# Attention on TensorE: kv products of two rows at once, 128 columns of k by 128 of v, of whose four quarters two are used

## The chip, the cores and the metric

One core of a Trainium2 chip runs the whole program. The metric is the device time of one execution in microseconds, as the median of several; every run is correct against the reference unless said otherwise. "Before" is the tuned kernel, "after" is the same kernel with the change. All times of single instructions are read from one profiled execution of each kernel.

## The reference, cut to what matters

```python
batch, n_heads, seq, head_dim = (8, 8, 576, 64)
...
kv = np.einsum('bhsd,bhse->bhde', k, v)          # the part that changes
out = np.einsum('bhsd,bhde->bhse', q, kv)
rms = np.sqrt(np.mean(out * out, axis=-1, keepdims=True) + 1e-06)
x = (out / rms * g_norm)                         # to (4608, 512)
# then: a gate, an assignment of tokens to 8 experts in order of their logits,
# and two matrix products per expert (512 -> 1024 -> 512) with a relu between
```

All of it is f32. For each batch and head, kv is a 64x64 matrix, the sum over 576 rows of the outer product of k and v.

## The kernel before

Two heads share the 128 partitions: partitions 0 to 63 (l=0) hold one, 64 to 127 (l=1) the other. A pair of heads is one r, and there are four r in a batch. The 576 rows of a head lie as 64 partitions by 9 rows j, so kv of a head is the sum of 9 matmuls with 64 rows, 64 columns of weights (k) and 64 moving columns (v). The output half is chosen by j, so that four products, 2 l by 2 parities of j, lie in four different 64x64 quarters of the array (in the trace, records of 64x64 that start in fours, 6 to 7 ns apart). The parts of even and odd j are added afterwards.

```python
        kv_ps = psa.tile([P, 2, 512], FT, name="kv_ps", tag="kv")
        def fill(times):      # keeps PE busy, its result is not used
            for _ in range(times):
                nc.tensor.matmul(kv_ps[:, 0, NP * D:512], lhsT=ones_b, rhs=wide[:, 0:512 - NP * D], start=True, stop=True)
        for r in range(NP):
            if r == 2:
                fill(10)
            for j in range(R):
                for l in range(2):
                    ls, cs = slice(l * D, (l + 1) * D), slice(j % 2 * D, (j % 2 + 1) * D)
                    nc.tensor.matmul(kv_ps[cs, l, r * D:(r + 1) * D], lhsT=k_sb[ls, r, j, :], rhs=v_sb[ls, r, j, :],
                                     start=(j < 2), stop=(j >= R - 2))
            if r < 2:
                turn_q(r)     # four transposes of q: the step qt_ps
                yield
        odd = att.tile([D, 2, NP * D], FT, name="odd", tag="odd")
        nc.scalar.copy(odd, kv_ps[D:P, :, 0:NP * D])
        kv = att.tile([D, NP, 2, D], FT, name="kv", tag="kv")
        nc.vector.tensor_tensor(kv..., kv_ps[0:D, :, 0:NP * D]..., odd..., op=AL.add)
        ...                   # t_ps: kv turned, w_ps: kv times the gate, kvx: both side by side
```

The loop that uses kv interleaves with this: for each tile of 128 tokens of batch b a step o_ps (eight matmuls, 64 rows, 128 columns of weights, 72 moving columns), then one piece of the work above for batch b + 1. One tile in nine (4 of 36) takes its two halves from two batches; there the weights are cut into two of 64 columns:

```python
                        parts = [(slice(0, P), halves[0], 2)] if halves[0][0] == halves[1][0] else [
                            (at[n], half, 1) for n, half in enumerate(halves)]
```

## Time and profile before

| | before |
|---|---|
| median time at first | 678.26 us (3 runs, 677.77 to 680.59) |
| span of the profiled run | 676.7 us |
| attention (from 20 us on PE busy 92.7 of 97 us, DMA share 0.92) | to about 117 us |
| search for the assignment (PE busy 18.8 of 46 us, mean clock 0.55) | about 117 to 163 us |
| MoE (PE busy 499.4 of 507 us to 670 us) | from 163 us |
| kv step of one r / of r=2 and 3 | 0.73 / 1.31 us |
| low clock (0.50) in the profiled run | 117.5 to 158.5 us, 3.4 us at 503 us, and the last 6 us |

The page of a profile gives each engine's busy share, digits for 40 slices of the span, and the chain that ended last: the work that, followed back from the end, made the time. The prediction below shows and reads the lines.

### The profile page before, as it was taken

Reading aid. Unit: us, or ns where it says so; the run is one execution under the profiler, and the core shown is the slowest. Engines: PE = TensorE matmul, PEld = TensorE weight load, DVE = VectorE, ACT = ScalarE, POOL = GpSimd, SP = SyncE. Lnnn points to the kernel's source line nnn. Section 1 sums busy time; section 2 is a strip of 40 time slices with the busy share of each in tenths; the row PEclk is TensorE's granted clock in tenths of the full one; section 3 lists DMA queues with packets and bytes.
Section 4 is the critical chain, followed back from the end, with each engine's and each line's share of the span. In section 5 each row is a group of like instructions: output and inputs, shape, how many; then the busy total and the mean of one; then the engine's idle time right before and its main releaser. Section 6 shows DMA issues by size and latency. Waiting matters only on the chain.

```text
span 676.7 us, 13040 instructions
## 1 busy us (share of the span) xinstructions
PE 625.0 (92%) x5123; PEld 488.7 (72%) x5123; DVE 439.9 (65%) x1418; ACT 171.7 (25%) x368; POOL 324.1 (48%) x319
## 2 busy tenths in 40 slices
PE   6999998338999999999999999999989999999994
PEld 4788787224778777877787787868767867887882
DVE  4564768888788888898888884678584155234311
ACT  1665665701210221022103110311123113112300
POOL 1054445002553546264508533846387559928622
PEclk9999999558999999999999999999989999999998
DMA  8999997207208207126207304510460343001002
GB/s 284 306 313 305 333 307 297 109 1 228 92 1 315 74 1 276 43 71 241 79 0 265 125 2 170 170 50 0 171 219 5 120 139 125 1 19 52 1 0 70
DMA packets 41405, 91.03 MB, mean 135 GB/s; under 512 B 3456, under 2 KB 3456, under 8 KB 41344
## 3 DMA queue, kind: packets, MB, share of 16 engines
q1 hardware_dynamic: 34752, 71.31, 30.5%
q0 software_dynamic: 5888, 18.88, 8.3%
q8 instruction: 40, 0.66, 0.4%
q14 instruction: 21, 0.17, 0.1%
q10 hardware_dynamic: 704, 0.02, 0.1%
HBM read 71.32 MB, written 18.87 MB: 133 GB/s over the span
## 4 chain that ended last, share of the span: by engine, by line
PE 82%; DVE 8%; issue 3%; POOL 3%; ACT 1%; DMA 1%; POOLq 0%; SPq 0%; DVEq 0%
PE y_ps L1022 28%; PE h_ps L972 22%; PE h_ps L915 8%; PE o_ps L398 5%; PE y_ps L1037 3%; PE kv_ps L335 3%; PE qt_ps L312 3%; PE t_ps L836 3%; PE kv_ps L327 2%; PE given_ps L558 1%; PE given_ps L554 1%; POOL tw L936 1%; DMA q_sb<-in_q_dram 1%; PE warm_ps L710 1%; DVE over_c L280 1%
## 5 line engine op out<-in xcount | busy, mean ns | idle before, releaser
L972 PE MATMUL h_ps<-xt,w_sb 128*128 128x256 f32 (+1 forms) x640 | 167.1, 412 | 0.1
L972 PEld LDWEIGHTS h_ps<-xt,w_sb 128*128 128x128 f32 x640 | 117.4, 190 | 32.3 <-issue 3.9
L1022 PE MATMUL y_ps<-tw,sh 128*128 128x256 f32 x384 | 86.8, 381 | 0.0
L1022 PEld LDWEIGHTS y_ps<-tw,sh 128*128 128x128 f32 x384 | 71.7, 190 | 9.1
L762 POOL DMA_INDIRECT xg<-x_dram,ids x40 | 38.1, 953 | 67.0 <-DVE held_ps L678 39.6
L950 POOL TENSOR_TENSOR sh<-hid 128x512 f32<-128x512 f32 x32 | 40.6, 1268 | 56.1 <-ACT hid L975 46.8
L975 ACT ACTIVATE hid<-h_ps 128x256 f32<-128x256 f32 (+1 forms) x80 | 32.8, 410 | 132.3 <-PE h_ps L972 124.1
L839 ACT ACTIVATE xt<-t_ps,g_col 128x512 f32<-128x512 f32 (+1 forms) x40 | 25.8, 644 | 143.1 <-PE t_ps L836 142.5
L264 DVE TENSOR_TENSOR over<-mx,held_ps 128x1152 bf16<-128x1152 f32 x42 | 56.9, 1354 | 1.6 <-issue 0.2
L1022 PE MATMUL y_ps<-w_sb,hid 128*128 128x256 f32 x256 | 57.7, 381 | 0.0
L1022 PEld LDWEIGHTS y_ps<-w_sb,hid 128*128 128x128 f32 x256 | 48.2, 190 | 7.0
L843 POOL DMA_INDIRECT out_dram<-y_sb,outs x32 | 32.6, 1020 | 40.8 <-DVE u L992 18.1
L999 POOL TENSOR_TENSOR y_sb<-u,u 128x512 f32<-128x512 f32 x8 | 10.1, 1266 | 78.5 <-issue 63.0
L427 POOL TENSOR_TENSOR xo<-o_sb,inv 128x512 f32<-128x512 f32 x31 | 33.0, 1094 | 28.5 <-ACT sq L404 15.5
L936 POOL TENSOR_TENSOR tw<-w_sb 128x512 f32<-128x512 f32 x32 | 39.9, 1271 | 11.9 <-DMA w_sb<-in_moe_w_dram 11.7
L992 DVE TENSOR_TENSOR y_sb<-y_ps,u 128x512 f32<-128x512 f32 x24 | 16.5, 688 | 39.3 <-PE y_ps L1022 39.1
L915 PE MATMUL h_ps<-sx,tv 128*128 128x288 f32 x144 | 41.2, 423 | 0.7 <-POOL tv L876 0.7
L600 DVE SCALAR_TENSOR_TENSOR held_ps<-n_full,held_ps 32x64 f32<-32x64 f32 x168 | 37.6, 224 | 5.7
L398 PE MATMUL o_ps<-kvx,qt 64*128 64x72 f32 (+1 forms) x640 | 38.7, 269 | 0.9 <-ACT o_sb L405 0.6
L398 PEld LDWEIGHTS o_ps<-kvx,qt 64*128 64x128 f32 (+1 forms) x640 | 33.7, 176 | 5.7 <-issue 2.9
L890 ACT ACTIVATE hid<-hid 128x288 f32<-128x288 f32 x48 | 21.2, 443 | 60.8 <-DVE hid L889 60.3
L992 DVE TENSOR_TENSOR u<-y_ps,u 128x512 f32<-128x512 f32 x24 | 16.4, 685 | 29.5 <-PE y_ps L1022 29.4
(232 smaller groups left out, 1089.2 us busy)
## 6 DMA issues: line engine op xcount, KB each, us to landing
w_sb<-in_moe_w_dram SPq DMA_DIRECT2D x16, 1024.0 KB, 6.2
w_sb<-in_moe_w_dram SPq DMA_DIRECT2D x8, 2048.0 KB, 16.2
k_sb<-in_k_dram SPq DMA_DIRECT2D x16, 576.0 KB, 5.8
v_sb<-in_v_dram SPq DMA_DIRECT2D x16, 576.0 KB, 5.8
q_sb<-in_q_dram SPq DMA_DIRECT2D x16, 576.0 KB, 5.5
x_dram<-xo SPq DMA_DIRECT2D x16, 512.0 KB, 4.1
x_dram<-xo SPq DMA_DIRECT2D x4, 256.0 KB, 4.5
xg<-x_dram,ids POOLq DMA_INDIRECT x40
```

The costliest lines, as they stand in the source:

```text
L264: nc.vector.tensor_tensor(over[:, c0:c1], mx[:, c0:c1].rearrange("p (c o) -> p c o", o=1).to_broadcast([P, c1 - c0, NCAND]), cand[:, 1:NCA ...
L398: nc.tensor.matmul(o_ps[rows_at, rp, (2 * r2 + l) * W:(2 * r2 + l + 1) * W], lhsT=turned_q[bn][ks, l, block // 2:block // 2 + m].rearrange ...
L427: nc.gpsimd.tensor_tensor(xo[:, t], o_sb[:, t, :, 0:D], inv[:, t * H:(t + 1) * H].rearrange("p (h o) -> p h o", o=1).to_broadcast([P, H, D ...
L600: nc.vector.scalar_tensor_tensor(some[g * QP:(g + 1) * QP], in0=n_full.to_broadcast([QP, 2 * QP]), scalar=0.5, in1=one_more, op0=AL.is_gt, ...
L762: tokens = nc.gpsimd.indirect_dma_start(out=xg[0:nr], out_offset=None, in_=x_dram, in_offset=bass.IndirectOffsetOnAxis(ap=ids[0:nr, n:n + ...
L915: nc.tensor.matmul(p_ps, lhsT=left[:, d], rhs=right[:, d], start=d == 0, stop=d == 1)
L936: in_order(nc.gpsimd.tensor_tensor(o[:, m:m + 2], x[:, m:m + 2], y[:, m:m + 2], op=AL.subtract))
L950: in_order(nc.gpsimd.tensor_tensor(o[:, ms], x[:, ms], y[:, ms], op=op))
L972: nc.tensor.matmul(h_ps, lhsT=w1[:, 2 * (d % 2) + d // 2, f * P:(f + 1) * P], rhs=xt[:, d, cs], start=(d == 0), stop=(d == DC - 1))
L975: nc.scalar.activation(hid[:, f, cs], h_ps, ACT.Relu)
L992: nc.vector.tensor_tensor(o, p_ps, u, op=AL.add)
L1022: nc.tensor.matmul(p_ps[:, n], lhsT=left[:, f, n * P:(n + 1) * P], rhs=right[:, f], start=(f == 0), stop=(f == FH - 1))
```

## The change

The intent is fewer and larger matmuls: two rows j at once, so that the weights are 128 columns (k of j and j+1) and 128 columns of v stream through. The output is 128x128; its upper left quarter is k_j by v_j, its lower right k_(j+1) by v_(j+1), and the other two quarters mix rows and are not used. There are nine rows, so row 8 stays alone, put in the middle of the sequence to let the first and the last product cover the whole output. The 18 matmuls of an r become 10, the trace's 1152 kv records 640.

```diff
         def fill(times):
             for _ in range(times):
-                nc.tensor.matmul(kv_ps[:, 0, NP * D:512], lhsT=ones_b, rhs=wide[:, 0:512 - NP * D], start=True, stop=True)
+                nc.tensor.matmul(kv_ps[:, 0, 2 * P:512], lhsT=ones_b, rhs=wide[:, 0:512 - 2 * P], start=True, stop=True)
 ...
-            for j in range(R):
+            for j in (0, 2, 8, 4, 6):
+                m = min(2, R - j)
                 for l in range(2):
-                    ls, cs = slice(l * D, (l + 1) * D), slice(j % 2 * D, (j % 2 + 1) * D)
-                    nc.tensor.matmul(kv_ps[cs, l, r * D:(r + 1) * D], lhsT=k_sb[ls, r, j, :], rhs=v_sb[ls, r, j, :],
-                                     start=(j < 2), stop=(j >= R - 2))
+                    ls = slice(l * D, (l + 1) * D)
+                    nc.tensor.matmul(kv_ps[0:m * D, l, r * P:r * P + m * D],
+                                     lhsT=k_sb[ls, r, j:j + m, :].rearrange("p j d -> p (j d)"),
+                                     rhs=v_sb[ls, r, j:j + m, :].rearrange("p j d -> p (j d)"),
+                                     start=(j == 0), stop=(j == 6))
 ...
-        odd = att.tile([D, 2, NP * D], FT, name="odd", tag="odd")
-        nc.scalar.copy(odd, kv_ps[D:P, :, 0:NP * D])
+        odd = att.tile([D, 2, NP, D], FT, name="odd", tag="odd")
+        kv4 = kv_ps.rearrange("p l (r c) -> p l r c", c=P)
+        nc.scalar.copy(odd, kv4[D:P, :, :, D:P])
 ...     (the addition reads kv4[0:D, :, :, 0:D])
```

More of the change, by code (lines that the diff above doesn't have):

```diff
@@ L339, in prepare @@
                 yield
-        odd = att.tile([D, 2, NP * D], FT, name="odd", tag="odd")
-        nc.scalar.copy(odd, kv_ps[D:P, :, 0:NP * D])
+        odd = att.tile([D, 2, NP, D], FT, name="odd", tag="odd")
+        kv4 = kv_ps.rearrange("p l (r c) -> p l r c", c=P)
+        nc.scalar.copy(odd, kv4[D:P, :, :, D:P])
         kv = att.tile([D, NP, 2, D], FT, name="kv", tag="kv")
         nc.vector.tensor_tensor(kv.rearrange("p r l d -> p l r d"),
-                                kv_ps[0:D, :, 0:NP * D].rearrange("p l (r d) -> p l r d", d=D),
-                                odd.rearrange("p l (r d) -> p l r d", d=D), op=AL.add)
+                                kv4[0:D, :, :, 0:D], odd, op=AL.add)
         kvx = att.tile([P, H, W], FT, name="kvx", tag="kvx", bufs=3)
```

## The prediction

> **What bounds the kernel now.** I read the page first, then cut out the stage that the change touches.
>
> ```profile
> span 676.7 us, 13040 instructions
> ...
> PE 625.0 (92%) x5123; PEld 488.7 (72%) x5123; DVE 439.9 (65%) x1418; ACT 171.7 (25%) x368; POOL 324.1 (48%) x319
> ...
> PEclk9999999558999999999999999999989999999998
> DMA  8999997207208207126207304510460343001002
> ...
> PE 82%; DVE 8%; issue 3%; POOL 3%; ACT 1%; DMA 1%; POOLq 0%; SPq 0%; DVEq 0%
> ```
>
> PE carries 82% of the chain that ended last. Each of the 40 slices is 16.9 us. The clock drops in slices 8 and 9, the serial search after attention, so attention is the first seven slices, to about 120 us. There the DMA digits are 8 and 9 as well, so two things could set that stage's pace. The table by stretch and the list of waits for its steady part tell them apart:
>
> ```profile
> 20.00:110.00 90.00, 86.69 (x1882) 73.39 (x1879) 57.93 (x128) 52.05 (x102) 37.19 (x41) 1.00 0.93 313
> ```
>
> ```profile
> PE qt_ps L312 <- ACT kvt L356: 2.1, 4, 0.5
> PE qt_ps L312 <- DVE kvx L365: 1.0, 3, 0.3
> ```
>
> The columns of the first are PE, weight load, DVE, ACT and POOL busy, clock, DMA share, GB/s. PE is busy for 86.7 of 90 us at full clock. It waits some 3 us for ACT and DVE and practically never for a transfer, although the DMA engines are 93% busy. So PE sets the pace, and time added to it lengthens the stage. The chain in order of time shows what its steps take:
>
> ```profile
> 42.16 0.66 PE o_ps L398 x32
> ...
> 45.18 1.04 PE o_ps L398 x16
> 46.23 0.73 PE kv_ps L335 x36
> 46.95 0.59 PE qt_ps L312 x4
> 47.54 1.05 PE o_ps L398 x16
> 48.59 0.73 PE kv_ps L335 x36
> ...
> 50.95 1.20 PE kv_ps L327 x10
> 52.15 1.31 PE kv_ps L335 x70
> ```
>
> Every f32 matmul of the code is two records: 18 products per r are the 36 of a kv step. A step of one r takes 0.73 us and the step of r=2 and r=3 together 1.31 us (70 of its 72 are counted). The o_ps lines are a ready-made test. The 32 records with 64x64 weights take 0.66 us, 21 ns each, while 16 with 64-row, 128-column weights take 1.04 us, 65 ns each, though both stream 72 columns. The change turns kv from the first kind into the second.
>
> The start times of single records give the periods. Four kv records (two row halves by two column halves) start 6 to 7 ns apart, then nothing for the rest of 58 ns. The wide o_ps records start in pairs every 112 ns. The f32 matmuls with 256 moving columns in the MoE start every 216 ns. Where the shape of the weights changes from one step to the next, the gap from the last start to the next step's first is 149 ns after kv and 202 ns after wide o_ps, instead of 58 and 112; the first period of the new step is then about 50 ns too long as well (107 for kv, 160 for wide o_ps). So a change of shape costs about 90 + 50 ns.
>
> [...]
>
> **The change, part by part.**
>
> *Moving and loading.* Before, a pair of rows j in both halves l is 4 products, 8 records, two groups of 58 ns: 117 ns. After, it is 2 products, 4 records, two pairs. Each pair streams 128 columns. 256 columns took 216 ns, so 128 take about 110 (estimate)[...]. [...] I take [...] the period of the wide o_ps, 112 ns. Two of these are 224 ns. Half of each product is thrown away, and the cost shows it: 107 ns more per pair of rows, 4 pairs per r. The lone row j=8 stays two groups of 58.
>
> *Changes of shape.* The built program gives the wide products a tile of 64x128 and the lone row one of 64x64, in the middle of every r. That adds two changes of shape per r. In exchange, a kv step before or after a wide o_ps step no longer has a change there.
>
> *A step of r=0 or r=1*, between o_ps and q's transposes: 3 gaps of 112, then 202 into the lone row, 107, 149 out of it, 160 + 112 + 112, and 202 to the transposes = 1380 ns. Before it was 729. The o_ps before it ends with 112 instead of 202. Net +561.
>
> *The step of r=2 and r=3*, from the filling matmuls to o_ps: (160 + 112 + 112) + 202 + (107 + 149) + (160 + 6 x 112) + 202 + (107 + 149) + (160 + 112 + 112 to o_ps) = 2628 ns. Before: 1313. The o_ps after it starts with a period of 112 instead of 160. Net +1267.
>
> *Sum.* A batch gains 2 x 561 + 1267 = 2389 ns; seven batches 16.7 us. In batch 0 the first r lies in front of 1.9 us of waiting for q and costs nothing, the others come to about 2.1 us (no o_ps beside them). That makes 18.8 us of PE time. From it I take 1 us: in three batches PE waits 0.4 us for the DVE copy of the last kvx columns, which a DVE with more time may have done sooner. The copies that take kv out have the same 512 elements and keep their 0.58 and 0.68 us. The filling matmuls stay, still 256 columns. Everything after attention, search and MoE, starts later by what attention gains. At its end DVE is on the chain, but its first piece there waits for ACT, and that for PE, so it has no backlog to hide a delay.
>
> 678.3 + 17.8 = **696 us**, 2.6% slower.
>
> **Rivals.**
>
> *Fewer instructions win.* 1152 kv records become 640. If issue were the limit (1152 records in 22.2 us, 19 ns each), kv would fall to 12.4 us and the kernel to 668. Against it: within a group four start in 20 ns and then PE pauses; it waits for columns, not for issue.
>
> [...] Then a batch gains 2 x 283 + 711 = 1277 ns, in all some 9 us with batch 0 and the deduction: 687. Against it: o_ps and kv, also 64x128 and 64x64, do pay when they meet.
>
> *Load and stream one after the other* in the wide tile: [...] this is my main risk upward.
>
> *Transfers hide it.* If DMA at 93% were the real bound, PE would have slack and the time would stay at 678. Against it: PE hardly waits for a transfer after 18 us.
>
> **Range and chances.** The base is firm (82% PE chain, no slack); the terms are +13.7 us from moving columns and +5 from shape changes less savings. [...] with periods of 120 instead of 112 it is 698. I take 688 to 701. The limit of 2% is 691.8, so: slower 0.85, within 2% 0.13, faster 0.02.
>
> **What would show it.** In the profile after: the kv step of one r at about 1.4 us in the chain instead of 0.73, that of two at about 2.6; pairs of wide records 112 ns apart; gaps of about 200 and 150 ns around each lone row; PE still some 96% busy in attention, DMA share down to about 0.8; the low clock and the search shifted by 17 to 18 us, everything later unchanged. [...] a longer PE step with an unchanged end of attention would say that something else was the bound, and I would be wrong altogether.

## The result, and the profile after

The changed kernel takes 701.09 us (median of 4 runs, 699.96 to 706.87), the kernel before 679.42 us on the same occasions (677.77 to 683.27). The ratio is 1.0328, 95% interval 1.0254 to 1.0401. Ratios here are the mean time of one kernel's fast runs over that of the other's fast runs of the same rounds, so they are not quite the ratio of the medians. Executions over 1.5% slower than the fastest of the same kernel are left out of the means. All outputs are right. The prediction, 696 us, had the direction and most of the size; the time lies just above its range of 688 to 701.

The page of the profile after:

```profile
span 699.8 us, 12015 instructions
...
PE 650.0 (93%) x4610; PEld 507.3 (72%) x4611; DVE 439.4 (63%) x1418; ACT 171.9 (25%) x368; POOL 324.0 (46%) x319
...
PEclk9899999955799999999999999999999999999998
DMA  8966789330530820801800910730162315002001
...
PE 83%; DVE 8%; POOL 3%; issue 2%; ACT 1%; DMA 1%; POOLq 0%; SPq 0%; DVEq 0%
```

There are 513 fewer PE matmul records, but PE is busy 25 us longer. The DMA digits of attention fall from 9 to between 6 and 9: the transfers now have time to spare. The second digit of the clock is an 8, which was a 9 before; more on it below. The table of the steady part of attention, to 125 us because attention is longer, with the same columns as in the prediction:

```profile
20.00:125.00 105.00, 102.04 (x1362) 84.66 (x1364) 53.40 (x123) 50.46 (x99) 33.54 (x37) 0.97 0.79 272
```

PE is busy 102 of 105 us, so it is still the bound, and the DMA share went from 0.93 to 0.79. The chain in order of time, for one batch:

```profile
56.27 1.05 PE o_ps L401 x16
57.32 1.40 PE kv_ps L336 x20
58.72 0.59 PE qt_ps L311 x4
...
63.38 1.20 PE kv_ps L327 x10
64.58 2.91 PE kv_ps L336 x40
67.48 0.88 PE o_ps L401 x15
```

The kv step of one r took 0.73 us and takes 1.40; that of two r took 1.31 and takes 2.91. The chain cuts at the modelled ends of records, which moves some 0.1 us between neighbours. From the first start of a step to that of the next, the three are 1.50, 2.81 and, for the o_ps step that follows the double one, 0.95 us instead of 1.05; it now follows a step of its own shape. The account further down uses these start times. The two copies that take kv out kept their 0.58 and 0.68 us.

Where the 23.2 us between the two profiled runs (676.7 and 699.8) lie is read from the first start of the step w_ps, which comes once per batch:

| part | longer by |
|---|---|
| start to w_ps of batch 0 (17.0 to 19.9 us) | 2.9 us |
| seven batches (93.1 to 114.9 us), without the low clock | 19.1 us |
| the low clock from 20.5 to 27.3 us, in the first of these | 2.6 us |
| from the last w_ps to the end (566.6 to 565.1 us) | -1.5 us |

The split of the seven batches uses another profiled run of the same kernel (after_again, below), in which that stretch has no low clock and takes 112.2 us. The last line is the 3.4 us of half clock at 503 us, which the run before had and the run after had not.

### The profile page after: what moved, and what is told of

Read it like the earlier page. It is cut to its first block, busy times and chain, and to the rows that moved or that the text cites.

```text
span 699.8 us, 12015 instructions
## 1 busy us (share of the span) xinstructions
PE 650.0 (93%) x4610; PEld 507.3 (72%) x4611; DVE 439.4 (63%) x1418; ACT 171.9 (25%) x368; POOL 324.0 (46%) x319
## 4 chain that ended last, share of the span: by engine, by line
PE 83%; DVE 8%; POOL 3%; issue 2%; ACT 1%; DMA 1%; POOLq 0%; SPq 0%; DVEq 0%
PE y_ps L1025 27%; PE h_ps L975 21%; PE h_ps L918 8%; PE kv_ps L336 7%; PE o_ps L401 4%; PE y_ps L1040 4%; PE qt_ps L311 3%; PE t_ps L839 3%; PE kv_ps L327 2%; PE given_ps L561 1%; PE given_ps L557 1%; POOL tw L939 1%; DMA q_sb<-in_q_dram 1%; PE warm_ps L713 1%; DVE over_c L280 1%
## 5 line engine op out<-in xcount | busy, mean ns | idle before, releaser
L336 PE MATMUL kv_ps<-v_sb,k_sb 64*128 64x128 f32 (+1 forms) x640 | 50.2, 286 | 0.3 <-DMA v_sb<-in_v_dram 0.3
L336 PEld LDWEIGHTS kv_ps<-v_sb,k_sb 64*128 64x128 f32 (+1 forms) x640 | 40.3, 180 | 9.2 <-issue 3.0
L352 POOL COPY kvx<-kv 64x512 f32<-64x512 f32 x16 | 9.7, 606 | 70.4 <-DVE kv L347 69.9
L918 PE MATMUL h_ps<-sx,tv 128*128 128x288 f32 x144 | 39.5, 409 | 0.7 <-POOL tv L879 0.7
```

What stands on the lines that cost most here:

```text
L336: nc.tensor.matmul(kv_ps[0:m * D, l, r * P:r * P + m * D], lhsT=k_sb[ls, r, j:j + m, :].rearrange("p j d -> p (j d)"), rhs=v_sb[ls, r, j:j ...
L918: nc.tensor.matmul(p_ps, lhsT=left[:, d], rhs=right[:, d], start=d == 0, stop=d == 1)
```

## The experiments

"lone row" is j=8. Runs 1 to 4 have four executions each and wide intervals that partly overlap; against the 2% limit the record calls all four unclear. So their step times in the traces carry the readings, and the medians only agree with them.

### 1. lone_wide: no change of shape inside an r

```diff
             for j in (0, 2, 8, 4, 6):
-                m = min(2, R - j)
+                j0, n = (j, 2) if j < 8 else (7, 1)
 ...
-                    nc.tensor.matmul(kv_ps[0:m * D, l, r * P:r * P + m * D],
-                                     lhsT=k_sb[ls, r, j:j + m, :]..., rhs=v_sb[ls, r, j:j + m, :]...
+                    nc.tensor.matmul(kv_ps[0:P, l, (r + 1) * P - n * D:(r + 1) * P],
+                                     lhsT=k_sb[ls, r, j0:j0 + 2, :]..., rhs=v_sb[ls, r, j:j + n, :]...
```

> The changed kernel with one thing altered: the lone row j=8 no longer uses a 64x64 tile. It takes the 128 columns of k of rows 7 and 8 as weights and streams v of row 8 only, into the right half of the output, so every kv product has the shape 64x128. Theory A [...]: its two pairs of records now cost 112 ns each instead of 58, but the gaps of 202 and 149 ns and the long first period of 213 ns in every r disappear. From the trace of the changed kernel, a step of one r goes from 1498 to about 158 + 8 x 112 + 202 = 1256 ns, the step of two from 2809 to about 213 + 18 x 112 + 105 = 2334: 0.96 us less per batch, 7.4 us in all, so about 694 us. Theory B (only the doubled moving columns cost): loading 128 columns instead of 64 for the lone row adds 2 x 54 ns per r, so 1.7 to 3.5 us more, about 703 us. Theory C (the surplus over the prediction came from a drop of the clock): no change, 701 us.

Measured: 693.84 us (4 runs), ratio to before 1.0222 (1.0113 to 1.0331). The chain of this kernel, one r and two:

```profile
54.74 1.16 PE kv_ps L336 x20
...
61.53 2.43 PE kv_ps L336 x40
```

These are 1.40 and 2.91 in the changed kernel. The lone row's four records now do more work (128 columns of weights instead of 64), and yet the step is 0.24 us shorter. By start times the two steps are 1261 and 2335 ns, for an expected 1256 and 2334. So changing the shape in the middle of an r costs time by itself (1.40 us a step against 1.16), as theory A says, and B falls. C falls as the whole cause: this profile has a low clock too (19.7 to 26.5 us), and the kernel is still faster.

### 2. narrow_weights: only the moving columns doubled

```diff
-            for j in (0, 2, 8, 4, 6):
-                m = min(2, R - j)
+            for j in (0, 1, 2, 3, 8, 4, 5, 6, 7):
+                h, n = j % 2, (2 if j < 8 else 1)
 ...
+                    nc.tensor.matmul(kv_ps[h * D:(h + 1) * D, l, r * P:r * P + n * D],
+                                     lhsT=k_sb[ls, r, j, :], rhs=v_sb[ls, r, j - h:j - h + n, :]...,
+                                     start=(j < 2), stop=(j in (6, 7)))
```

> Weights as before the change (64 columns, 64x64 tiles, four at a time, no change of shape inside an r), but each streams 128 columns of v, of which 64 are used. It isolates the doubled moving columns. Theory A: four records start every 112 ns instead of every 58, the lone row stays at 58 per pair[...]. A step of one r is about 1150 ns (729 before the change), the step of two about 2160 (1313): 1.7 us more per batch than before the change, 13.6 us in all, about 692 us, 9 us less than the changed kernel. Theory B (wide weights or their loads are what costs, not the columns streamed): the groups of four stay at 58 to 65 ns and the time near 680 us. Theory D (half as many instructions matter): it has as many records as before the change, so it should be slower than the changed kernel, above 701 us.

Measured: 692.34 us (4 runs), ratio 1.0166 (1.0084 to 1.0247). The chain:

```profile
53.84 1.14 PE kv_ps L336 x34
...
60.57 2.13 PE kv_ps L336 x68
```

Theory A had 1.15 and 2.16. The first period after a change of shape was 160 ns. By the start times of single records, groups of four start every 110 ns where they started every 58 before the change, with the same weights and the same number of records (72 for two r, of which the chain counts 68). So the streamed columns alone cost 11 to 13 us (by the ratio, and against the 679.4 us of before), although half of the results are thrown away. That the load does not matter is not shown by this: the wide o_ps has a period of 112 ns with only 72 streamed columns, so doubling the weights alone may have been enough as well; no run tried it on kv. Theory D, that the number of instructions matters, falls: this kernel has 1152 kv records and is faster than the one with 640.

### 3. two_visits: twice as many changes of shape

```diff
-            for j in (0, 2, 8, 4, 6):
+            for j, halves in ((0, (0, 1)), (8, (0,)), (2, (0, 1)), (4, (0, 1)), (8, (1,)), (6, (0, 1))):
                 m = min(2, R - j)
-                for l in range(2):
+                for l in halves:
```

> The changed kernel with its suspected cost doubled: the lone row's product of the lower half stands after the first pair of rows, that of the upper half after the third, so PE changes the shape four times per r instead of twice, with the same products. Theory A: one more visit per r costs (202 - 112) to leave the wide shape, 107 + 149 in the lone row, and (213 - 112) to come back: about 447 ns, less what the lone records lose in the first visit (nothing, as two records took two periods before too); 31 times, 14 us, so about 715 us. Theory B or C: the same records and columns, so 701 us.

Measured: 724.57 us (4 runs, 718.92 to 727.68), ratio 1.0617 (1.0509 to 1.0725). The chain:

```profile
71.36 1.85 PE kv_ps L336 x20
...
79.52 3.80 PE kv_ps L336 x40
```

One r is 0.45 us longer than in the changed kernel, as expected (447 ns), and two are 0.89 longer. The interval from one w_ps to the next is 17.67 or 17.82 us instead of 15.88 or 16.04: 1.79 us per batch, which is 4 x 447 ns. Eight batches are 14.3 us. The median is 23 us up, and its profile shows where some of the rest is: the clock is low from 9.9 to 16.7 us and from 23.6 to 44.0 us. In the second of these the interval takes 26.1 us instead of 17.7. The mean clock of its four runs is 0.944 to 0.955, against 0.954 to 0.966 for the changed kernel. So in the profiled run the expected 715 us was missed for the clock, not for the visits; for the other three the clock is the likely cause.

### 4. after_no_fill: is PE time still kernel time?

```diff
             if r == 2:
-                fill(10)
+                fill(0)
```

> The changed kernel without the ten filling matmuls ahead of r=2 in each batch. It asks whether PE time still turns into kernel time one to one after the change, now that the DMA share in attention is 0.79 instead of 0.93. Theory A (PE alone sets the pace): 1.2 us less per batch, 8 x 1.2 = 9.6 us, about 691.5 us. Rival E (transfers are close behind PE): less than half of that comes, above 696 us, with waits of PE for k, v or q. [...]

Measured: 691.1 us (4 runs, 688.93 to 699.13), ratio 1.0179 (1.0055 to 1.0303). It is what theory A had (691.5). Every batch is 1.35 us shorter (14.54 or 14.68 us), a little more than the fillers' own 1.20. A change of shape goes with them: in the trace after, the gap from o_ps into them is 211 ns and kv behind them starts with a period of 213, where kv straight behind o_ps has 112 and 158, which makes the other 0.15 us (estimate from these four). Its DMA share is 0.84 between 20 and 125 us. After the change PE alone sets the pace, and time saved on it comes back in full.

### 5 and 6. after_warm and after_warm_again: the low clock at 20 us

The same kernel was submitted twice, the second time beside an unaltered changed kernel, after_again.

```diff
+        def warm(times):
+            if b == 0:
+                w_ps = psa.tile([P, 2, 512], FT, name="warm_o", tag="o", bufs=2)
+                for _ in range(times):
+                    nc.tensor.matmul(w_ps[:, 0, 0:256], lhsT=ones_b, rhs=wide[:, 0:256], start=True, stop=True)
 ...
         turn_q(2)
+        warm(8)
         t_ps = psa.tile(...)
 ...
+        warm(4)
         turn_q(3)
 ...
         turn_q(4)
+        warm(5)
```

> The changed kernel with 17 small filling matmuls (256 columns, 110 ns each) in the three pauses of PE in batch 0: eight while kv is taken out, four while its transpose is copied, five before the first o_ps; they write a PSUM buffer of o_ps that is not yet in use. It tests Theory C, that part of the surplus over the prediction is a drop of the clock to half for 6.8 us at 20 us (the trace of the changed kernel has it, the trace before does not; the second batch took 19.1 us instead of 16.0). Theory C: no low clock before 130 us, second batch 16.0 us, median about 698 us with less spread. If the drop does not hang on these pauses, it stays and the time is 701 us, or 0.5 us more if the fillers do not fit into the pauses.

Measured: 699.75 us (4 runs, 697.35 to 700.52), ratio 1.0327 (1.0279 to 1.0374). Its profile has no low clock before 142 us, and the first interval between two w_ps is 16.45 us instead of 19.10. Its median is 1.3 us below that of the changed kernel, its ratio the same.

> The changed kernel once more, unaltered, so that it stands beside the next run on the same chip with the same runs of the kernel before. Ratio to before 1.03 to 1.035. If the low clock at 20 us is part of the change, its profile shows it again and most of its runs have a mean clock of 0.962 or less; if it is chance, the profile may lack it and the runs spread from 0.955 to 0.968.

Measured: 700.95 us (6 runs, 697.62 to 711.62, of which two are slow), ratio 1.0293 (1.0229 to 1.0358). Its profile has a low clock again, but at another time, from 8.9 to 15.7 us, where it makes batch 0 2.8 us longer (w_ps at 22.69 us instead of 19.89). The mean clock of its four fast runs is 0.961, 0.963, 0.966 and 0.968, that of the slow ones 0.945 and 0.947.

> The changed kernel with fillers in the pauses of batch 0, with more rounds. If the early drop of the clock costs about 3 us in most runs and the fillers prevent it, this is 2 to 3 us faster than the unaltered changed kernel beside it. If the drop is chance and rare, the two agree within 1 us, and the missing microseconds of the prediction are in the periods alone.

Measured: 699.77 us (6 runs, 697.36 to 700.71), ratio 1.0291 (1.0243 to 1.0339), and no low clock before 139 us in its profile. Two of two profiles with fillers lack the early low clock, two of two without have it, and the spread is smaller with them; but the ratios of the fast runs agree, 1.0291 and 1.0293. So in the profiles of after and after_again an early low clock of 6.8 us cost 2.6 and 2.8 us; how often it occurs in runs that are not profiled stays open, and on the mean of the fast runs no difference was found. The other profiles lean the same way. All six of the changed kernel and its variants without these fillers (after, after_again and runs 1 to 4) have a low stretch that starts between 8.9 and 20.5 us, and none of the three of before, before_no_fill and before_fill5 has one before 80 us. (Runs 9 and 10, made from the kernel before, have early ones too, from 25.9 and 9.8 us.) So the change may favour it; neither the profiles nor the times prove it.

### 7. before_no_fill: how far PE was the bound before

```diff
             if r == 2:
-                fill(10)
+                fill(0)
```

> The kernel before the change without its ten filling matmuls ahead of r=2. It asks how far PE was the bound before, when the DMA share in attention was 0.93. Theory A (PE alone): 8 x 1.2 = 9.6 us less, 669 us. Rival E (transfers are just behind PE): PE now waits for k, v or q; less than half of the gain comes, 674 to 679 us, DMA share 0.95 or more[...].

Measured: 676.0 us (20 runs, of which five are slow, 669.87 to 694.65), before 679.46 (30 runs), ratio 0.9921 (0.9889 to 0.9953). The table of the steady part:

```profile
20.00:105.00 85.00, 81.05 (x1733) 69.29 (x1734) 53.71 (x121) 49.44 (x98) 34.68 (x38) 0.92 0.93 311
```

Most batches are shorter than before, four of seven by about 1.0 to 1.6 us, but the mean clock fell to 0.92: from 80.5 to 94.2 us it is low, and one batch takes 17.75 us. The four best runs, with a mean clock of 0.962 to 0.964, take 669.87 to 670.96 us, close to the 669 of theory A; by the ratio the gain is 5.4 us (0.79% of 679). Transfers did not take over: the DMA share is 0.93 as before, and no wait for k, v or q is in the list of PE's waits. What took the rest was the clock: with the fillers gone, it drops in more of the runs. A mean clock of 0.957 or more stands in 7 of these 20 runs and in 24 of the 30 of before.

### 8. before_fill5: half of them

```diff
             if r == 2:
-                fill(10)
+                fill(5)
```

> The kernel before the change with five filling matmuls ahead of r=2 instead of ten: half the PE time given back (8 x 0.55 = 4.4 us), fewer waits and clock drops than without any. PE as the only bound: 4.4 us less, ratio 0.9935. [...] This is the candidate for a version that beats both kernels; it is expected to stay within 2% of the kernel before.

Measured: 674.79 us (22 runs, of which one is slow, 671.49 to 681.76), before 679.35 (27 runs), ratio 0.9937 (0.9907 to 0.9966). The profiled run spans 670.4 us, has no low clock before 117 us, and most of its batches take 0.55 us less. It is the fastest by its median of all that were tried, and beats both kernels, the one before by 0.6% only. By the ratio of fast runs before_no_fill is its equal (0.9921, overlapping intervals).

### 9 and 10. before_split_o and before_split_o_no_fill: the opposite edit, at o_ps

```diff
-                        parts = [(slice(0, P), halves[0], 2)] if halves[0][0] == halves[1][0] else [
-                            (at[n], half, 1) for n, half in enumerate(halves)]
+                        parts = [(at[n], half, 1) for n, half in enumerate(halves)]
```

> The kernel before the change, with the opposite edit made to o_ps: its 64x128 weights are cut into two halves of 64 columns, so that four 64x64 tiles work at once and o_ps has the shape of kv. In the trace the tiles that are already cut take 0.66 us for 32 records, the wide ones 1.04 us for 16. Theory A: 31 tiles save 0.38 us each and the change of shape to kv and back goes (about 0.14 us, some 15 times): 14 us less, 665 us, if PE alone is the bound. Rival E: transfers take over, and only 3 to 6 us come. If the shape does not matter, 679 us.

Measured: 689.71 us (4 runs, 687.43 to 692.53), ratio 1.0163 (1.0105 to 1.0222): slower, where 665 was expected from theory A. The steps themselves are as fast as expected: o_ps takes 0.55 us from its start to kv's start where nothing disturbs it, instead of 1.05. But PE's waits between 18 and 115 us and the table say:

```profile
PE kv_ps L335 <- issue: 7.4, 5, 2.8
PE o_ps L397 <- issue: 6.0, 4, 2.7
```

```profile
20.00:105.00 85.00, 69.83 (x1824) 56.95 (x1817) 42.36 (x100) 40.98 (x81) 27.11 (x30) 0.84 0.80 271
```

PE stands still for 13.4 us in nine stretches, the longest 2.8 us, in the middle of a step and for nothing that the profile shows ("issue"), and the clock falls to 0.84 on average. It is not rival E: the DMA share is 0.80, less than before. In the trace, the four stretches of over 2 us (from 22.48, 45.48, 58.07 and 88.68 us) each have a packet of the queue q8 that starts within 0.5 us of the stretch's start (22.04, 45.56, 58.45, 88.96). Each lasts until 1.2 to 1.6 us after that packet is through. The page of the profile lists q8 under "instruction": 40, 36 and 44 packets, 0.66, 0.59 and 0.72 MB, for before, after and this kernel, so 16 KiB a packet. With 5123, 4610 and 5635 matmul records that makes 128 bytes a record in each of the three. From this proportion I take it that q8 brings PE's instructions (estimate). That PE ran out of instructions is my reading of the coincidence; no run takes it apart. The traces do show more than four cases. Between 20 and 118 us the four runs before_no_fill, before_fill5, before_split_o and before_split_o_no_fill have 22 stops of PE of more than 0.2 us that are put down to issue. Every one ends 1.2 to 1.6 us after a packet of q8 is through, though not every packet has a stop. The traces of before and after have no such stop there.

> Both edits to the kernel before the change: o_ps in 64x64 tiles and no ten filling matmuls. Theory A: 14 + 9.6 us less, 655 us. Rival E: no further gain over the better of the two single edits, because the loads of k, v and q at some 310 GB/s set the pace[...].

Measured: 685.71 us (11 runs, 680.31 to 689.39), ratio 1.0109 (1.0073 to 1.0146). It gains 4 us on the split alone by the medians and stays slower than before. Its clock is low in six stretches between 9 and 106 us (0.930 to 0.952 on the mean of each run). Neither theory had this.

## Why the prediction was right or wrong

**The bound** was right. PE was busy 96% of the steady part before and 97% after, and what the fillers gave back (10 us by the medians, 1.35 us per batch) shows that PE time became kernel time. That transfers could hide it is out: their share fell.

**Moving columns** were right. Wide pairs start every 112 ns in the trace after, and narrow_weights, which doubles them alone, has steps of 1.14 and 2.13 us for an expected 1.15 and 2.16. That its median is 692.3 us for an expected 692 is in part luck, as the interval of its ratio is 11 us wide.

**Changes of shape** were right in kind. The gaps around the lone row are 202 and 149 ns, as taken from the kernel before; lone_wide took them away and gained 7 us, two_visits doubled them and paid 1.79 us per batch. (These two count from the last record of a group. From its first record, as the periods of 58 and 112 do, they are 208 and 156, so a change adds about 97 ns and not 90.)

**The step that failed** is "160 + 112 + 112": the first period of a wide kv step after a change of shape. I took 160 ns over from the wide o_ps. That step loads the same 128 columns but streams 72, and kv streams 128. The trace after has 207 ns. Both count from the second record of the first pair; from its first record they are 167 and 213. Counted so, the first period after a change of shape is made up alike in the five measured cases of kv and o_ps. In the traces before and after, the first matmul of a step starts 2 ns after its weight load. The second load starts 55 ns after the first where it has 64 columns and 108 or 109 ns where it has 128, and the second matmul starts 53 to 54 ns after the second load where it streams 64 columns, 60 where it streams 72 and 107 where it streams 128. Old kv has 55 + 53 - 2 (107 ns measured), the o_ps in the old cut form 55 + 60 - 2 (113), wide o_ps 108 + 60 - 2 (167), wide kv 108 + 107 - 2 (213); narrow_weights would have 55 + 107 - 2, and its trace has 160. So in the first period load and stream stand one after the other. In the later periods, 58 ns for old kv, 110 for narrow_weights and 112 for wide o_ps and wide kv, they do not. The sums are read off these starts; no run isolates why they hold. The term enters five times per batch, once in each of the single steps and three times in the double one; 5 x 47 ns are 0.24 us, more than half of the 0.34 us that a batch misses.

**A neighbour of it** failed too: kv after o_ps of the same shape was to start with a period of 112 ns and starts with 158. In the trace its second load begins only 48 to 50 ns after the start of its first matmul, and the second matmul starts 109 ns after that load, which together are the 158. The single step took 1498 ns where 1380 was predicted, the double one 2809 where it was 2628. Against it stands the o_ps after kv, which became 102 ns shorter instead of 48. But then kv was not ready to be turned, and PE waits 0.1 us per batch for the addition on DVE; the list of waits of the weight loads after shows it, and in it the row of the wait that I had meant to disappear:

```profile
PEld t_ps L357 <- DVE kv L347: 1.8, 7, 0.3
...
PEld qt_ps L311 <- DVE kvx L368: 1.3, 3, 0.4
```

For PE itself this second wait was 1.0 us in three times before, and it is 1.0 us in three times after.

**The deduction of 1 us** was thus wrong: DVE starts that copy when w_ps is done, not when it has time (in the trace before it waits for w_ps 4.4 us in six times between 20 and 110 us), so a slower PE didn't shorten the wait. What did vanish is one pause of 0.4 us inside an o_ps step, at 54 us in the trace before. It ends 1.25 us after a packet of q8 is through, like the stops of run 9.

**The sum.** The seven intervals had 16.7 us predicted and show 19.1; batch 0 had 2.1 and shows 2.9, of which 0.5 is a first kv that starts later in this run (7.27 us instead of 6.79; unchanged kv code also started at 7.67 us in before_no_fill); the deduction of 1.0 did not come. That makes 22.0 us instead of 17.8, and the medians differ by 21.7. The low clock of 2.6 us and the 1.5 us the other way, which only the profiled pair shows, are left out of this sum, so the close match is partly chance.

**The working.** Three slips of the prediction are small. Its sums add gaps counted from a pair's last record to periods counted from the first, and so lose 6 or 7 ns per change of shape, about 0.1 us per batch. The terms printed for the double step come to 2516 ns; the total of 2628 is right, with one more period of 112 before o_ps. The 12.4 us of the first rival is 12.3.

**The rivals.** "Fewer instructions win" is out by narrow_weights. The second, that wide and lone products follow each other at no extra cost, is out by lone_wide (0.24 us less per single step) and two_visits (0.45 us more). "Load and stream one after the other" is out as a rule for every period, as wide kv starts every 112 ns, but it is what the starts show in the first one (213 ns): a part of this rival, which I had called my main risk upward, is what was missing. A low clock, which I had not thought of as a rival, cost 2.6 and 2.8 us in the profiles of after and after_again, but the mean of the fast runs does not show that the change brings it on, though the profiles lean that way.

## What to carry to other kernels

Before merging small products into a larger one of which part is thrown away, count columns and loads per tile of the array, not instructions: here four 64x64 tiles finish four useful products in 117 ns, and two 64x128 tiles need 224 ns for the same four, because each loads and streams twice the columns, and either alone came with such a period (110 ns with 64 columns loaded and 128 streamed in narrow_weights, 112 with 128 loaded and 72 streamed in wide o_ps). Count the changes of tile shape in the order in which they stand on PE; each cost about 97 ns here before the next step started, plus a longer first period (213 ns instead of 112 for wide kv, 107 instead of 58 for old kv), and giving a leftover product the shape of its neighbours can be cheaper than giving it less work (1.16 us a step in lone_wide, 1.40 in the changed kernel). When a duration is taken over from another step as a model, check that both its load and its stream have the new step's size: the first period of wide o_ps, with 72 columns streamed, was 167 ns, that of wide kv, with 128, was 213.
